# A sliding-window attention fused with a hard-swish MLP: a written TensorE order, one exp per block type, and a padded last tile

## The chip, the core and the metric

The kernel runs on one core of a Trainium2 chip. A core has TensorE (PE) for matrix products, VectorE (DVE), ScalarE (ACT) and GpSimd (POOL) for element-wise work, and SyncE (SP), which here only issues transfers between device memory and on-chip memory. Each engine works off its own queue in order. TensorE writes to psum, from which ACT and VectorE read. The metric is the device time of one execution in microseconds.

## The reference

Eight batches, eight heads, 576 positions, head size 64. Each position attends to itself and the 127 before it, with a bias that falls with the distance. The result, 4608 tokens of 512 values, goes through two matrix products with h * clip(h + 3, 0, 6) / 6 between them.

```python
scores = scale * np.matmul(q, k.transpose(0, 1, 3, 2))          # (8, 8, 576, 576)
mask = (rel >= 0) & (rel < window)                              # window = 128
scores = np.where(mask, scores + bias[None], -1000000000.0)
attn = np.exp(scores - np.max(scores, axis=-1, keepdims=True))
attn = attn / (np.sum(attn, axis=-1, keepdims=True) + 1e-09)
x = np.matmul(attn, v) ...                                      # (4608, 512)
h = x @ w_in                                                    # (4608, 2048)
g = h * np.clip(h + 3.0, 0.0, 6.0) / 6.0
return g @ w_out                                                # (4608, 512), float32
```

## The kernel before

The 576 positions are cut in tiles of 128; the fifth, last tile has 64 rows. With a window of 128, a tile of keys meets only its own tile of queries (the diagonal block) and the next one (the off-diagonal block). The unit of attention is a head pair: two heads fill the 128 partitions, 64 each. There are 32 pairs (8 batches of 4).

For a batch, SP loads q, k and v in 15 transfers (L80), POOL casts them to bf16 (L114 to L118). For a pair, TensorE transposes q and k (L127, 10 matmuls against an identity) and VectorE copies them out of psum (L130). Then two halves follow. In each TensorE makes scores (L142, L148: transposed, keys on partitions), diagonal and off-diagonal block of a key tile in one matmul of 256 columns; ACT takes the exp per block type (L159 to L169), two blocks of a type at once where it can, six passes to a head; POOL sets what lies outside the window to zero (L173 to L187); TensorE multiplies with v (L201 to L208), where v has a column of ones, so that column 64 is the sum; VectorE takes the reciprocal and multiplies (L213, L214). At last TensorE transposes the pair's result back (L223) and VectorE copies it into xT (L225), which holds all tokens with the model dimension on partitions.

The MLP (called MoE in the code) works on 9 groups of 512 tokens. An "up" (L235) is four matmuls of 512 columns, followed by a relu on ACT (L239) and a min-and-multiply on VectorE, which gives g (L240). A "down" (L251) is four matmuls of 512 columns from the group before, and every fourth down ends a tile of the output, which ACT or VectorE copies out of psum (L256, L258) and SP stores. There are 16 ups and 16 downs to a group; "unit" stands below for either.

The program writes attention of batch 0 first. Then it goes through the groups, and after each step's up and down it takes some pieces of the next batch's attention, by a generator that yields after each piece (L261 to L279). A scheduler then sets the order in each engine's queue and takes the liberty to move instructions past each other. In psum there are one score buffer (two banks), one av buffer, two transpose buffers, two up buffers (hps) and one down buffer (ops).

Of the kernel before, what the change touches and what calls it, by code (L numbers as in the profile page):

```python
# [18 lines left out]
def kernel(  # L19
# [18 lines left out]
    LAST = S - 4 * 128  # L38
    W = D + 1
# [18 lines left out]
    casts = ctx.enter_context(tc.tile_pool(name="casts", bufs=2))  # L58
    vpool = ctx.enter_context(tc.tile_pool(name="vpool", bufs=1))
    qkt = ctx.enter_context(tc.tile_pool(name="qkt", bufs=3))  # L60
    ppool = ctx.enter_context(tc.tile_pool(name="ppool", bufs=4))
    small = ctx.enter_context(tc.tile_pool(name="small", bufs=4))
    gpool = ctx.enter_context(tc.tile_pool(name="gpool", bufs=2))
    rpool = ctx.enter_context(tc.tile_pool(name="rpool", bufs=3))
    opool = ctx.enter_context(tc.tile_pool(name="opool", bufs=4))
# [5 lines left out]

    vbuf = [vpool.tile([128, NQ, H, W], BF16, name=f"vbuf{i}") for i in range(2)]

    def load(b):
        got = []
        for src, nm in ((q, "qf"), (k, "kf"), (v, "vf")):
            t = loads.tile([128, NQ, H, D], FP32, tag="ld", name=nm)
            for j in range(NQ):
                n = min(128, S - j * 128)
                nc.sync.dma_start(  # L80
                    out=t[:n, j, :, :],
                    in_=src[b, :, ds(j * 128, n), :].rearrange("h p d -> p h d"))
            got.append(t)
        return got

    first = load(0)
# [10 lines left out]
    for t in vbuf:  # L97
        nc.vector.memset(t[:, :, :, D:W], 1.0)

    for ks in range(n_ks):  # L100
        nc.gpsimd.dma_start(out=w_in_sb[:, ks, :], in_=moe_w_in[ts(ks, 128), :])
    for g in range(4):
        nc.gpsimd.dma_start(
            out=w_out_sb[:, ts(g, 4), :],
            in_=moe_w_out[ds(g * 512, 512), :].rearrange("(m p) d -> p m d", p=128))

    def attention(b):
        qf, kf, vf = first if b == 0 else load(b)
        qb = casts.tile([128, NQ, H * D], BF16, name="qb")
        kb = casts.tile([128, NQ, H * D], BF16, name="kb")  # L110
        vb = vbuf[b % 2]
        for src, dst in ((qf, qb), (kf, kb)):
            s = src.rearrange("p j h d -> p j (h d)")
            nc.gpsimd.tensor_copy(out=dst[:, 0:4, :], in_=s[:, 0:4, :])  # L114
            nc.gpsimd.tensor_copy(out=dst[:LAST, 4, :], in_=s[:LAST, 4, :])
        nc.gpsimd.tensor_copy(out=vb[:, 0:4, :, 0:D].rearrange("p j h d -> p (j h) d"),
                              in_=vf[:, 0:4, :, :].rearrange("p j h d -> p (j h) d"))
        nc.gpsimd.tensor_copy(out=vb[:LAST, 4, :, 0:D], in_=vf[:LAST, 4, :, :])  # L118
        yield

        for hp in range(NP):
            qkT = []
            for src, nm in ((qb, "qT"), (kb, "kT")):
                tp = ps_tp.tile([128, S], BF16, tag="tp", name="tp")
                for j in range(NQ):
                    n = min(128, S - j * 128)
                    nc.tensor.transpose(tp[:, ds(j * 128, n)], src[:n, j, ts(hp, 128)],  # L127
                                        ident[:n, :n])
                t = qkt.tile([128, S], BF16, tag=nm, name=nm)
                nc.vector.tensor_copy(out=t, in_=tp)  # L130
                qkT.append(t)
                yield
            qT, kT = qkT
            pt = []
            avs = small.tile([128, NQ, 2, D], BF16, tag="avs", name="avs")
            for st in range(2):
                sc = ps_sc.tile([128, 2, 512], FP32, tag="sc", name="sc")
# [123 lines left out]
    for _ in attention(0):  # L261
        pass
# [47 lines left out]
```

## Time and profile before

| | |
|---|---|
| median of 3 runs | 478.93 us (477.62 to 479.73) |
| the profiled execution | 478.99 us, span of its instructions 477.3 us |
| TensorE, matmuls | 403.3 us busy, 85% of the span, 2528 of them |
| VectorE, ACT, POOL | 41%, 46%, 32% |
| MoE up, MoE down | 576 matmuls of 512 columns each |

The span is the time from the first to the last instruction of the program. Matmuls are pipelined: one of 512 columns is shown with 0.38 us and the next starts 0.22 us later, so what a matmul costs is read from starts, not from durations.

### The profile page before, as it was taken

The page shows a single profiled execution, that of the slowest core. Times are in us where ns is not written, and L with a number is a line of the kernel's source. Part 1 is how long each engine was busy: PE and PEld are TensorE (multiplying, and loading weights), DVE is VectorE, ACT ScalarE, POOL GpSimd, SP SyncE. Part 2 cuts the span into 40 slices and gives each one's busy share as a digit, 9 for nine tenths or more (in the row PEclk, how much of TensorE's full clock was granted, in tenths as well). Part 3 has the DMA queues.
Part 4 walks back from the last instruction along what each step waited for, and adds up shares of the span by engine and source line. Part 5 has one row for each costly group of instructions (what it writes and reads, how often), then busy time and mean ns, then how long its engine had stood idle before and what let it go on. Part 6 is the DMA issues. An engine that isn't in the chain of part 4 may idle for free. (4 is left out here: it accounts for less than half of the span.)

```text
span 477.3 us, 6932 instructions
## 1 busy us (share of the span) xinstructions
PE 403.3 (85%) x2528; PEld 187.2 (39%) x2528; DVE 194.5 (41%) x470; ACT 219.9 (46%) x547; POOL 150.4 (32%) x255
## 2 busy tenths in 40 slices
PE   0003775998999999999999999999999999999976
PEld 0001432444344444444444444444444444444432
DVE  1000333554355545444544454454444544443420
ACT  1002335566565465546554655555545564444410
POOL 5025644454533622462245225522222222000000
PEclk9999999999799999999999999999999999999999
DMA  8999999500926877669409200000000000101111
GB/s 157 200 205 194 197 198 191 101 0 1 188 66 115 160 146 129 126 143 163 83 23 186 57 23 23 23 22 24 23 23 23 22 23 23 46 22 45 44 45 66
DMA packets 120419, 42.39 MB, mean 89 GB/s; under 512 B 113217, under 2 KB 115265, under 8 KB 120385
## 3 DMA queue, kind: packets, MB, share of 16 engines
q1 hardware_dynamic: 117696, 37.76, 40.8%
q0 software_dynamic: 2688, 4.19, 5.0%
q8 instruction: 19, 0.31, 0.3%
q14 instruction: 16, 0.12, 0.1%
HBM read 36.70 MB, written 9.44 MB: 97 GB/s over the span
## 5 line engine op out<-in xcount | busy, mean ns | idle before, releaser
L235 PE MATMUL hps<-xT,w_in_sb 128*128 128x512 bf16 x576 | 159.6, 388 | 3.3 <-DVE xT L225 2.1
L239 ACT ACTIVATE r<-hps,bias 128x512 f32<-128x512 f32 x144 | 98.2, 692 | 135.2 <-PE hps L235 135.0
L251 PE MATMUL ops<-w_out_sb,g 128*128 128x512 bf16 x576 | 155.0, 383 | 3.4 <-DVE osb L258 2.0
L240 DVE SCALAR_TENSOR_TENSOR g<-r,hps 128x512 bf16<-128x512 f32 x144 | 97.7, 683 | 114.1 <-ACT r L239 112.8
L173 POOL TENSOR_SCALAR_AFFINE_SELECT pp<-pp 128x512 bf16<-128x512 bf16 x64 | 40.6, 634 | 211.2 <-ACT pp L159 106.9
L159 ACT ACTIVATE pp<-sc,bias_d 128x256 bf16<-128x256 f32 x128 | 60.4, 472 | 99.2 <-PE sc L142 54.3
L251 PEld LDWEIGHTS <-g 128*128 128x128 bf16 x576 | 52.6, 98 | 62.3 <-issue 8.0
L235 PEld LDWEIGHTS <-w_in_sb 128*128 128x128 bf16 x576 | 51.3, 98 | 56.2 <-issue 8.3
L201 PE MATMUL av<-vbuf,pp 128*128 128x65 bf16 (+1 forms) x256 | 44.0, 208 | 5.3 <-DVE avs L214 2.9
L127 PE MATMUL tp<-ident,qb 128*128 128x128 bf16 (+1 forms) x160 | 21.9, 227 | 30.5 <-POOL qb L114 29.1
L205 PE MATMUL av<-vbuf,pp 128*128 128x65 bf16 x256 | 33.7, 203 | 14.2 <-POOL pp L173 11.6
L213 DVE RECIPROCAL rc<-av 128x4 f32<-128x4 f32 (+1 forms) x96 | 16.6, 172 | 69.0 <-PE av L208 49.5
L142 PE MATMUL sc<-qT,kT 64*128 64x256 bf16 (+1 forms) x256 | 35.0, 290 | 5.6 <-ACT pp L162 3.4
L214 DVE TENSOR_TENSOR avs<-av,rc 128x256 bf16<-128x256 f32 (+1 forms) x96 | 35.8, 372 | 1.4
L130 DVE COPY qT<-tp 128x576 bf16<-128x576 bf16 x32 | 14.5, 453 | 45.9 <-PE tp L127 45.8
L201 PEld LDWEIGHTS <-pp 128*128 128x128 bf16 (+1 forms) x256 | 23.3, 103 | 23.4 <-POOL pp L178 6.6
L205 PEld LDWEIGHTS <-pp 128*128 128x128 bf16 x256 | 19.8, 101 | 30.4 <-POOL pp L173 28.7
L162 ACT ACTIVATE pp<-sc,bias_o 128x256 bf16<-128x256 f32 x64 | 30.4, 476 | 0.0
L127 PEld LDWEIGHTS <-qb 128*128 128x128 bf16 (+1 forms) x160 | 12.8, 102 | 35.2 <-POOL qb L114 29.1
L223 PE MATMUL tp<-ident,avs 128*128 128x128 bf16 (+1 forms) x160 | 25.4, 226 | 0.0
L127 PE MATMUL tp<-ident,kb 128*128 128x128 bf16 (+1 forms) x160 | 19.2, 226 | 7.2 <-POOL kb L114 6.5
L142 PEld LDWEIGHTS <-kT 64*128 64x128 bf16 x256 | 10.6, 96 | 34.4 <-issue 19.6
(37 smaller groups left out, 294.7 us busy)
## 6 DMA issues: line engine op xcount, KB each, us to landing
out_dram<-osb SPq DMA_DIRECT2D x36, 256.0 KB, 2.0
qf<-in_q_dram SPq DMA_DIRECT2D x32, 256.0 KB, 5.3
kf<-in_k_dram SPq DMA_DIRECT2D x32, 256.0 KB, 5.1
vf<-in_v_dram SPq DMA_DIRECT2D x32, 256.0 KB, 5.0
w_in_sb<-in_moe_w_in_dram POOLq DMA_DIRECT2D x4, 512.0 KB, 10.6
w_out_sb<-in_moe_w_out_dram POOLq DMA_DIRECT2D x4, 512.0 KB, 20.6
qf<-in_q_dram SPq DMA_DIRECT2D x8, 128.0 KB, 5.0
kf<-in_k_dram SPq DMA_DIRECT2D x8, 128.0 KB, 5.4
```

Source lines behind the costliest of these rows:

```text
L127: nc.tensor.transpose(tp[:, ds(j * 128, n)], src[:n, j, ts(hp, 128)], ident[:n, :n])
L142: nc.tensor.matmul(sc[:, e, ds(j * 256, n)], lhsT=kT[e * D:(e + 1) * D, ts(kt, 128)], rhs=qT[e * D:(e + 1) * D, ds(kt * 128, n)], start=Tr ...
L159: nc.scalar.activation(out=pp[:, e, :, 0:128], in_=s4[:, :, 0:128], func=ACT.Exp, bias=bias_d[:, h:h + 1], scale=scale)
L162: nc.scalar.activation(out=pp[:, e, :, 128:256], in_=s4[:, :, 128:256], func=ACT.Exp, bias=bias_o[:, h:h + 1], scale=scale)
L173: nc.gpsimd.affine_select(out=dg, in_=dg, pattern=[[0, 4], [1, 128]], channel_multiplier=-1, base=0, compare_op=ALU.is_ge, fill=0.0)
L201: nc.tensor.matmul(av[:m, i, e, :], lhsT=src, rhs=vb[:, qt - 1, h, :], start=True, stop=False)
L205: nc.tensor.matmul(av[:m, i, e, :], lhsT=src, rhs=vb[:, qt, h, :], start=(qt == 0), stop=True)
L214: nc.vector.tensor_tensor(out=avs[:m, qts[lo]:qts[lo] + n, :, :], in0=av[:m, lo:lo + n, :, 0:D], in1=rc[:m, lo:lo + n, :, :].to_broadcast( ...
L235: nc.tensor.matmul(hps, lhsT=w_in_sb[:, ks, ts(ms, 128)], rhs=xT[:, ks, ts(nt, NT)], start=(ks == 0), stop=(ks == n_ks - 1))
L239: nc.scalar.activation(out=r6, in_=hps, func=ACT.Relu, bias=bias3[:, 0:1], scale=1.0 / 6.0)
L240: nc.vector.scalar_tensor_tensor(out=gts[nt][:, ms, :], in0=r6, scalar=1.0, in1=hps, op0=ALU.min, op1=ALU.mult)
L251: nc.tensor.matmul(ops[nt, sub], lhsT=gts[nt][:, ms, ts(sub, 128)], rhs=w_out_sb[:, ms, :], start=(ms == 0), stop=(ms == n_ms - 1))
```

## The change

On TensorE the order is now the program's own (`manual_schedule`); the other engines are scheduled as before. A loop over the 32 pairs and one more writes it: pieces of pair g (diagonal scores, off-diagonal scores), of pair g + 1 (transposes) and of pair g - 1 (values, transposing back), with eight units between them (`fill`). A unit is written only if its tokens' attention has been written before it; else `fill` returns with nothing. So no unit comes in the iterations 0 to 3, two ups at the end of 4, eight ups in 5, six in 6, none in 7, two units at the end of 8, and eight in each of the iterations 9 to 32. After the loop, 78 units are left.

Scores are made per block type: all four diagonal blocks of both heads (8 matmuls of 128 columns), later all off-diagonal ones with the last tile's own 64 columns (10 matmuls). So one exp of 512 columns serves a head's blocks of a type, and one of 64 columns the last tile. The last tile of q, k, v and of its probabilities is padded to 128 rows in buffers that are set up once, so that all transposes and value matmuls are 128 by 128. Values are taken for query tiles 0 to 2 and then 3 and 4. Batch 0 is loaded pair by pair (12 transfers each) and cast on VectorE; w_in is loaded by columns, in front of POOL's first selects, and w_out behind them. Pools of r6 and output buffers shrink to two.

In the rows of order below, a name on the left of `<-` is written. This is VectorE's queue before, at about the third batch: g is the product after an up, rc and avs belong to values, qT, kT and xT are copies out of the transpose buffers.

```order
L225 COPY xT<-tp 128x576
L240 SCALAR_TENSOR_TENSOR g<-r_2052,hps 128x512
L240 SCALAR_TENSOR_TENSOR g<-r_2077,hps 128x512
L213 RECIPROCAL rc<-av 128x4
L214 TENSOR_TENSOR avs<-av,rc 128x256
L258 COPY osb<-ops 128x512
L240 SCALAR_TENSOR_TENSOR g<-r_2116,hps 128x512
L213 RECIPROCAL rc<-av 128x4
L214 TENSOR_TENSOR avs<-av,rc 128x256
L213 RECIPROCAL rc<-av 64x2
L214 TENSOR_TENSOR avs<-av,rc 64x128
L130 COPY qT<-tp 128x576
```

And the same engine now, over one iteration in the same part of the program:

```order
L258 SCALAR_TENSOR_TENSOR g<-r_1997,hps 128x512
L258 SCALAR_TENSOR_TENSOR g<-r_2030,hps 128x512
L230 RECIPROCAL rc<-av 128x6
L231 TENSOR_TENSOR avs<-av,rc 128x384
L258 SCALAR_TENSOR_TENSOR g<-r_2057,hps 128x512
L230 RECIPROCAL rc<-av 128x4
L231 TENSOR_TENSOR avs<-av,rc 128x256
L158 COPY qT<-tp 128x640
L158 COPY kT<-tp 128x640
L258 SCALAR_TENSOR_TENSOR g<-r_2100,hps 128x512
L242 COPY xT<-tp 128x576
L258 SCALAR_TENSOR_TENSOR g<-r_2138,hps 128x512
```

A pair's values are now two pieces, of 384 and 256 elements, where they were three; one g stands ahead of each reciprocal. The next place is POOL's queue at the start, before:

```order
L101 DMA w_in_sb<-in_moe_w_in_dram 128x2048 x4
L103 DMA w_out_sb<-in_moe_w_out_dram 128x4x512 x4
L114 CAST qb<-qf 128x2048
L115 CAST qb<-qf 64x512
L114 CAST kb<-kf 128x2048
L115 CAST kb<-kf 64x512
L116 CAST vbuf_109<-vf 128x32x64
L118 CAST vbuf_109<-vf 64x8x64
L173 AFFINE_SELECT pp<-pp 128x4x128
```

And now:

```order
L119 DMA w_in_sb<-in_moe_w_in_dram 128x4x512 x4
L176 AFFINE_SELECT pd<-pd 128x512 x2
L204 AFFINE_SELECT po<-po 128x512
L125 DMA w_out_sb<-in_moe_w_out_dram 128x4x512
L204 AFFINE_SELECT po<-po 128x512
L207 AFFINE_SELECT p4buf_112<-p4buf_112 128x2x64
L125 DMA w_out_sb<-in_moe_w_out_dram 128x4x512
L176 AFFINE_SELECT pd<-pd 128x512 x2
L125 DMA w_out_sb<-in_moe_w_out_dram 128x4x512
L204 AFFINE_SELECT po<-po 128x512 x2
```

The casts of batch 0 have left POOL, and the four loads of w_out stand between the selects of the first two pairs.

```diff
+    def load_pair(got, b, hp):
+        for nm, src in srcs:
+            for h in (2 * hp, 2 * hp + 1):
+                nc.sync.dma_start(out=got[nm][:, 0:4, h, :],
+                                  in_=src[b, h, 0:512, :].rearrange("(t p) d -> p t d", p=128))
+                nc.sync.dma_start(out=got[nm][:LAST, 4, h, :], in_=src[b, h, 512:S, :])
...
+    for i in range(2):
+        nc.vector.memset(vbuf[i][:, :, :, D:W], 1.0)
+        nc.vector.memset(vbuf[i][64:128, 4, :, 0:D], 0.0)
+        nc.vector.memset(qbuf[i][64:128, 4, :], 0.0)
+        nc.vector.memset(kbuf[i][64:128, 4, :], 0.0)
+        nc.vector.memset(p4buf[i], 1.0)
...
+    def scores_diag(g):
...
+        for j in range(4):
+            for e in range(2):
+                r = slice(e * D, (e + 1) * D)
+                nc.tensor.matmul(sc[:, e, ts(j, 128)], lhsT=kT[r, ts(j, 128)],
+                                 rhs=qT[r, ts(j, 128)], start=True, stop=True)
+        pd = ppool.tile([128, 2, 4, 128], BF16, tag="pd", name="pd")
+        for e in range(2):
+            h = 2 * hp + e
+            nc.scalar.activation(out=pd[:, e, :, :].rearrange("p j c -> p (j c)"),
+                                 in_=sc[:, e, :], func=ACT.Exp,
+                                 bias=bias_d[:, h:h + 1], scale=scale)
...
+    def values(g, qts):
...
+        av = ps_av.tile([128, 3, 2, W], FP32, tag="av", name="av")
+        nq = len(qts)
+        for i, qt in enumerate(qts):
+            for e in range(2):
+                h = 2 * hp + e
+                if qt > 0:
+                    nc.tensor.matmul(av[:, i, e, :], lhsT=po[:, e, qt - 1, :],
+                                     rhs=vb[:, qt - 1, h, :], start=True, stop=False)
+                d = pd[:, e, qt, :] if qt < 4 else p4[:, e, :]
+                nc.tensor.matmul(av[:, i, e, :], lhsT=d, rhs=vb[:, qt, h, :],
+                                 start=(qt == 0), stop=True)
...
+    def fill(n):
+        for _ in range(n):
+            if at[0] == len(units):
+                return
+            nt, fn, step = units[at[0]]
+            if fn is moe_up and done[0] < NP * (min((nt * NT + NT - 1) // S, B - 1) + 1):
+                return
+            fn(nt if fn is moe_up else nt - 1, step)
+            at[0] += 1
...
+    with tc.manual_schedule(engines={mybir.EngineType.PE}):
+        prepare(0)
+        transposes(0)
+        for g in range(G + 1):
+            if g < G:
+                scores_diag(g)
+            if g + 1 < G:
+                prepare(g + 1)
+            fill(2)
+            if g > 0:
+                values(g - 1, (0, 1, 2))
+            fill(1)
+            if g > 0:
+                values(g - 1, (3, 4))
+            fill(1)
+            if g < G:
+                scores_off(g)
+            fill(1)
+            if g + 1 < G:
+                transposes(g + 1)
+            fill(1)
+            if g > 0:
+                back(g - 1)
+            fill(2)
+        fill(len(units))
```

`prepare(g)` casts pair g on VectorE in batch 0, casts a whole batch on POOL at the first pair of a later one, and writes the loads of the next batch at a batch's second pair.

## Rows read from the trace of the kernel before

**Rows 1.** The page: TensorE's busy share in 40 slices of 11.9 us, in tenths.
```profile
PE   0003775998999999999999999999999999999976
```
**Rows 2.** Timetable of POOL at the start: start us, duration us, instruction, idle before.
```profile
27.14 1.89 POOL L114 CAST qb<-qf 128x2048 bf16<-128x2048 f32 x1 [20.32 <-DMA qf<-in_q_dram]
30.48 0.61 POOL L115 CAST qb<-qf 64x512 bf16<-64x512 f32 x1 [1.45 <-DMA qf<-in_q_dram]
```
**Rows 3.** Timetable of SP's queue at the start: batch 0's q, batch 1's k.
```profile
0.81 15.76 SPq L80 DMA_DIRECT2D qf<-in_q_dram  x5
...
44.97 5.87 SPq L80 DMA_DIRECT2D kf<-in_k_dram  x5
```
**Rows 4.** Timetable of TensorE near the end of the second stage.
```profile
83.18 1.86 PE L235 MATMUL hps<-xT,w_in_sb 128*128 128x512 bf16 x4 [1.12 <-DVE g L240]
```
**Rows 5.** Busy time by stretch: length, PE, PEld, DVE, ACT, POOL; clock; DMA.
```profile
120.00:380.00 260.00, 251.00 (x1656) 116.97 (x1655) 125.88 (x303) 141.97 (x364) 93.41 (x161) 0.99 0.40 82
400.00:440.00 40.00, 40.00 (x186) 17.91 (x185) 17.60 (x29) 17.41 (x26) 0.00 (x0) 1.00 0.09 34
```
**Rows 6.** TensorE's groups from 120 to 380 us: count | busy us, mean ns.
```profile
L235 PE MATMUL hps<-xT,w_in_sb 128*128 128x512 bf16 x355 | 97.0, 383 | 0.0
L251 PE MATMUL ops<-w_out_sb,g 128*128 128x512 bf16 x344 | 96.2, 386 | 0.0
```
**Rows 7.** Timetable of TensorE in the steady stage.
```profile
204.09 0.39 PE L142 MATMUL sc<-qT,kT 64*128 64x256 bf16 x4
204.41 1.04 PE L235 MATMUL hps<-xT,w_in_sb 128*128 128x512 bf16 x4
...
210.04 0.20 PE L205 MATMUL av<-vbuf,pp 128*128 128x65 bf16 x1 [0.21 <-POOL pp L173]
210.08 0.20 PE L201 MATMUL av<-vbuf,pp 128*128 128x65 bf16 x1
...
211.25 0.22 PE L201 MATMUL av<-vbuf,pp 128*64 128x65 bf16 x1
211.40 0.21 PE L208 MATMUL av<-vbuf,p 64*64 64x65 bf16 x1
...
212.64 0.39 PE L127 MATMUL tp<-ident,qb 128*128 128x128 bf16 x4
212.86 0.28 PE L223 MATMUL tp<-ident,avs 128*128 128x128 bf16 x2
```
**Rows 8.** Timetable of ACT in the steady stage: an exp, a relu.
```profile
205.67 0.48 ACT L162 ACTIVATE pp<-sc,bias_o 128x256 bf16<-128x256 f32 x1
206.02 0.70 ACT L239 ACTIVATE r<-hps,bias 128x512 f32<-128x512 f32 x1
```
**Rows 9.** Timetable of VectorE in the steady stage: g, then a pair's last values.
```profile
210.48 0.69 DVE L240 SCALAR_TENSOR_TENSOR g<-r,hps 128x512 bf16<-128x512 f32 x1 [0.28 <-ACT r L239]
211.65 0.18 DVE L213 RECIPROCAL rc<-av 128x4 f32<-128x4 f32 x1 [0.49 <-PE av L208]
211.87 0.42 DVE L214 TENSOR_TENSOR avs<-av,rc 128x256 bf16<-128x256 f32 x1
```
**Rows 10.** The page: weight loads of the scores; loads of k.
```profile
L142 PEld LDWEIGHTS <-kT 64*128 64x128 bf16 x256 | 10.6, 96 | 34.4 <-issue 19.6 <-DVE kT L130 5.5 <-DVE xT L225 2.5
...
kf<-in_k_dram SPq DMA_DIRECT2D x32, 256.0 KB, 5.1
```
**Rows 11.** Stretch with TensorE alone: length, PE; clock; DMA.
```profile
122.00:124.00 2.00, 2.00 (x9) 0.50 1.28 257
```
**Rows 12.** The chain that ended last, its end: start us, us, what.
```profile
454.64 0.02 issue
...
456.72 3.63 PE ops L251 x16
...
461.01 3.63 PE ops L251 x16
...
473.34 0.69 DVE osb L258
```

More of the change, by code (lines that the diff above doesn't have):

```diff
@@ L38 @@
     LAST = S - 4 * 128
+    SP = NQ * 128
     W = D + 1
@@ L80, in load @@
                 nc.sync.dma_start(
-                    out=t[:n, j, :, :],
+                    out=got[nm][:n, j, :, :],
                     in_=src[b, :, ds(j * 128, n), :].rearrange("h p d -> p h d"))
-            got.append(t)
-        return got
-    first = load(0)
+    got0 = new_loads()
+    for hp in range(NP):
+        load_pair(got0, 0, hp)
     make_identity(nc, ident)
@@ L228, with transposes @@
-    gts = {}
+                              in_=got["vf"][:, 0:4, :, :].rearrange("p j h d -> p (j h) d"))
+        nc.gpsimd.tensor_copy(out=vb[:LAST, 4, :, 0:D], in_=got["vf"][:LAST, 4, :, :])
+    st = {}
+    def transposes(g):
+        b, hp = divmod(g, NP)
+        for src, nm in ((qbuf[b % 2], "qT"), (kbuf[b % 2], "kT")):
+            tp = ps_tp.tile([128, SP], BF16, tag="tp", name="tp")
+            for j in range(NQ):
+                nc.tensor.transpose(tp[:, ts(j, 128)], src[:, j, ts(hp, 128)], ident)
+            t = qkt.tile([128, SP], BF16, tag=nm, name=nm)
+            nc.vector.tensor_copy(out=t, in_=tp)
+            st[g, nm] = t
@@ new lines, in values @@
+    def values(g, qts):
+        b, hp = divmod(g, NP)
+        vb = vbuf[b % 2]
+        pd, po, p4 = st[g, "pd"], st[g, "po"], p4buf[g % 2]
+        av = ps_av.tile([128, 3, 2, W], FP32, tag="av", name="av")
+        nq = len(qts)
+        for i, qt in enumerate(qts):
+            for e in range(2):
+                h = 2 * hp + e
+                if qt > 0:
[4 more added lines that the diff above has]
+                                 start=(qt == 0), stop=True)
+        if qts[0] == 0:
+            st[g, "avs"] = small.tile([128, NQ, 2, D], BF16, tag="avs", name="avs")
+        rc = small.tile([128, 3, 2, 1], FP32, tag="rc", name="rc")
+        nc.vector.reciprocal(rc[:, 0:nq, :, :], av[:, 0:nq, :, D:W])
+        nc.vector.tensor_tensor(
+            out=st[g, "avs"][:, qts[0]:qts[0] + nq, :, :], in0=av[:, 0:nq, :, 0:D],
+            in1=rc[:, 0:nq, :, :].to_broadcast([128, nq, 2, D]), op=ALU.mult)
@@ L230, in moe_up, with back @@
+    def back(g):
+        b, hp = divmod(g, NP)
+        avs = st[g, "avs"]
+        tp = ps_tp.tile([128, SP], BF16, tag="tp", name="tp")
+        for j in range(NQ):
+            nc.tensor.transpose(tp[:, ts(j, 128)],
+                                avs[:, j, :, :].rearrange("p e d -> p (e d)"), ident)
+        nc.vector.tensor_copy(out=xT[:, hp, ds(b * S, S)], in_=tp[:, 0:S])
+        done[0] = g + 1
+    done = [0]
+    gts, ops = {}, {}
     def moe_up(nt, ms):
@@ L241, in moe_up @@
                                        op0=ALU.min, op1=ALU.mult)
-    ops = {}
     def moe_down(nt, step):
```

236 lines of the change are left out of this document (89 added, 147 removed).

## The prediction, made before the changed kernel was run

> **What bounds the kernel now.** I read the 40 slices first, then the timetables of the start, the groups by stage, and one steady stretch matmul by matmul. The slices show three stages [rows 1]: TensorE does nothing for some 29 us, works at 30 to 80% until about 85 us, and is at 90% or more to the end. In the first stage it waits for data: POOL's first cast waits 20.32 us for the DMA of q [rows 2], and SP needs 15.76 us to issue five loads beside the weight loads where 5.87 do later [rows 3]. In the second, head pairs run one after the other, and TensorE's clock is low: four 512-column matmuls last 1.86 us [rows 4], where four of the steady stage last 1.04 [rows 7].
>
> In the third stage TensorE is busy, but not full. A pure MoE stretch has 186 matmuls in 40.00 us [rows 5], 0.86 us per unit of four. From 120 to 380 us there are 1656 matmuls [rows 5], of which 355 + 344 = 699 are MoE [rows 6]. These are 175 units, 151 us; the other 109 us go to 957 attention matmuls. A head pair has 43 (15 transposes, 10 scores, 18 values), so 22.3 pairs at 4.9 us each. The timetable shows why [rows 7]: full value matmuls start 0.04 us apart and four full transposes take 0.22, but a value matmul of the 64-row last tile holds TensorE for 0.15; four score matmuls of 256 columns hold it for 0.32; and at 210.04 it has stood empty for POOL's select. The other engines are at 55% or less there [rows 5]. So the bound is TensorE's own order.
>
> **The change, part by part.** All durations are from the profiled execution (478.99 us, span 477.3), which lies on the median of 478.93.
>
> *TensorE's work for a pair.* 15 full transposes at 0.055 us are 0.8; 18 full value matmuls at 0.04 are 0.7 [rows 7]. Scores come in groups of 8 and 10, and two heads run side by side in 64 rows each. Two such steps of 256 columns hold 0.32 us; 512 columns of MoE alone are 0.215, so 0.1 is the change of shape on the way out, and I take as much on the way in. A step of 128 columns is then 0.055, rounded to 0.06; 7 of these, 2 short ones of 0.04 and two groups' changes of 0.2 give 0.9. The pair needs 2.4 us. Bounds for a score step are 0.04 (the pace of value matmuls) and 0.15 (that of the partial tile): 2.3 to 3.2 us. I take the row that it is nearest to, the 256-column step.
>
> Beside that row stands a rule. The Trainium skill (TensorE: Matmul & The Clock Gate, "Part 3: Packing small matmuls — row/col tiling", "The mechanism") says that a weight load overlaps running matmuls only when its row group differs. Every score step reloads both row groups; by this rule twice as many steps would bring their weight loads into the open, some 28 us over the run by the trace's length of a load.
>
> *Waits that the written order leaves.* One iteration holds eight units, 6.9 us, and one pair: diagonal scores, up, down, values 0 to 2, up, values 3 and 4, down, off-diagonal scores, up, transposes, down, back, up, down. Values 3 and 4 write the single av buffer, which VectorE must have read. After the diagonal scores ACT does two exps, then the first up's relu. An exp of 256 columns holds ACT for 0.35 us and lasts 0.48, a 512-wide pass lasts 0.70 [rows 8], so I estimate 0.57 for 512. The relu ends 2.3 us after the diagonal scores began, and VectorE's g (0.69 [rows 9]) ends at 3.0; in VectorE's queue g stands ahead of the reciprocal. The values are done at 2.6. Reciprocal and product take 0.22 + 0.42 us at 256 elements [rows 9], some 0.8 at 384, so av is free at 3.85, where values 3 and 4 are due at 3.3: 0.55 us of wait. The first down after a finished output tile waits some 0.2 us on average for the copy out of the one buffer, the first up of a batch about half a microsecond for xT. That is 0.9 per pair singly; as a wait gives time to the next, I take 0.8. The ends: nothing (VectorE free in time), and 2.5, which is what the pair holds now beyond its 2.4.
> What hides the rest: exps and selects have six units and the pieces between, some 6.4 us, before their values are asked for. POOL's casts (1.89 and 0.61 [rows 2]) can stand in between; with two of them the cover is gone.
> An iteration is 6.9 + 2.4 + 0.8 = 10.1 us, against 6.9 + 4.9 = 11.8 now.
>
> *The start.* The first pair is loaded by itself and cast on VectorE, and w_out is issued behind POOL's first selects, so TensorE starts well before 29 us. But in its order the transposes of batch 1 stand ahead of the last values of batch 0, and the first unit behind these. So k of batch 1 decides. The bytes ahead of it (q, k and v of batch 0, the weights, q of batch 1) are those of now; SP has issued it by 50.84 us [rows 3], and a load lands 5.1 after its issue [rows 10]: 55. With 48 transfers for batch 0 in place of 15 I allow 50 to 60. Then POOL casts (1.89 + 0.61), and transposes, diagonal scores, values 0 to 4, off-diagonal scores, transposes and back follow at the low clock, 7.5 us with their copies: the first unit starts at 65. Sixteen ups follow with two pairs: 13.8 us of matmuls, 4.8 for the pairs, 1.5 for the low clock, and six because an up's psum buffer (two) is held through relu (0.70) and g (0.69), so that ups alone come 1.28 us apart: 91. The next two pairs have no units, since the next up needs all of batch 1, and take their chain of exp, select, values and copy, 9 us for both; then two units: 102. The clock may fall there: it is granted at 0.50, 1.2 of 2.4 GHz, from 122 to 124 us now [rows 11]. I add 3 us for half the pace.
>
> *The end.* Ups and downs alternate strictly; the down behind a finished tile waits some 0.3 us for the copy at ten places: 3 us. The last 16 downs keep their waits, 456.72 - 454.64 = 2.1 us before them and 4.29 - 3.63 = 0.7 three times between [rows 12]: 4.1. From the last matmul at 473.34 to the span's end are 4.0, to the run's end 1.7 more.
>
> *Off the path.* Wider exps (ACT is at 55%), memsets (in the DMA wait), longer copies of the padded tile (VectorE is at 48% [rows 5]). If this cover goes, the wait above grows by what they add, under 0.2 us per pair.
>
> *Sum.* 102 + 3 + 24 iterations x 10.1 (242) - 2 for what the last two leave out + 78 units left x 0.86 (67) + 3 + 4.1 + 5.7 = 425. I take 421: the clock's 3 us are not certain, nor are all the singly added waits. Start 92 and wait 0.3 give about 400; start 107 and wait 1.4, 444.
>
> **Rivals.**
> 1. The waits hide. TensorE is then bound by its own 9.3 to 9.4 us per iteration: 24 x 0.75 less, 403. For it: VectorE is half idle. Against: one av buffer, and g ahead of the reciprocal.
> 2. The written order cannot step round a late producer, as a scheduler's can. With selects behind POOL's casts the values wait, and an iteration is 11.2 to 12: 447 to 466. For it: the cover that two casts use up. Against: the order puts casts one to three pairs ahead, and POOL's queue is a third busy [rows 5].
> 3. Weight loads in the open. Each of the 9 score steps pays one load, 96 ns by the mean [rows 10]: 0.86 x 32 = 28 us, 449. Against: at 204.09 two steps take little over the time of their columns, loads included, so these were hidden. The rule named above makes this rival; the trace so far speaks against it.
> 4. Slower. At each of the seven batch changes TensorE stands until the next batch is cast: three casts of 1.89 + 0.61 on POOL are 7.5 us, and the copies and scores behind them 1 more: 60 us in all, 481. It decides from 8.3 us per change. For it: POOL's queue stops at a cast whose load is late, and the transposes stand fast in TensorE's order. Against: a batch's loads are issued in 18 us (three times 5.87) of an iteration's four times 10.
>
> **How the numbers follow.** Forecast 0.58, rival 1 0.15, rival 2 0.18, rival 3 0.06, rival 4 0.03. The forecast's own range is 408 to 436; with most of rival 1 and half of 2 and 3 it is 400 to 446. Within 0.5% (2.4 us, about what a measurement can tell from no change) is 0.01; slower is rival 4, 0.03; faster 0.96.
>
> **What would show it.** Value matmuls 0.04 us apart to the last tile, score steps of 0.06, iterations of 10 us with one wait of half a microsecond before values 3 and 4 that VectorE's avs ends; the first MoE matmul at 60 to 70 us, behind the cast of batch 1's k; a stretch of some 9 us without MoE before 100. I am wrong on the start if the first MoE matmul comes before 55 or after 75, on the waits if TensorE stands before values 0 to 2 (POOL) or before ups, and on the work if score steps take over 0.1 us.

## The result, and the profile after

The median of four runs is 419.54 us (419.14 to 421.72), beside 478.27 us (477.28 to 479.73) for the kernel before: a ratio of 0.878, with a 95% interval of 0.874 to 0.882. The prediction was 421. The profiled execution took 419.74 us, its span 417.7.

The page of the kernel after, TensorE's 40 slices (10.4 us each) and busy time, which answers to [rows 1]:

```profile
PE   0141618878999899989998999899899999999985
...
PE 338.9 (81%) x2739; PEld 175.2 (42%) x2784; DVE 201.5 (48%) x438; ACT 198.5 (48%) x355; POOL 145.1 (35%) x217
```

TensorE starts earlier, stands at 10 to 60% until about 60 us, and behind that it is still the busiest engine but less full than it was: an 8 comes back every four slices or so.

TensorE's timetable of the kernel after at the start (start us, duration us, instruction, idle before):

```profile
8.95 0.72 PE L156 MATMUL tp<-ident,qbuf 128*128 128x128 bf16 x5 [8.95 <-DVE qbuf L132]
...
62.30 0.84 PE L156 MATMUL tp<-ident,kbuf 128*128 128x128 bf16 x5 [4.07 <-POOL kbuf L142]
...
69.19 2.60 PE L253 MATMUL hps<-xT,w_in_sb 128*128 128x512 bf16 x7 [0.22 <-issue]
...
91.90 0.40 PE L168 MATMUL sc<-qT,kT 64*128 64x128 bf16 x8
```

The first transposes come at 9 us instead of some 29, but the first unit only at 69.19: the transposes of batch 1's k at 62.30 stand ahead of it in the written order. At 91.90 begins the first of the two iterations without units.

POOL and SP of the kernel after at the start, which answer to [rows 2, 3]; first POOL, then SP:

```profile
60.35 1.89 POOL L142 CAST kbuf<-kf 128x2048 bf16<-128x2048 f32 x1 [2.46 <-DMA kf<-in_k_dram]
```

```profile
51.58 5.83 SPq L93 DMA_DIRECT2D kf<-in_k_dram  x5
```

The five loads of batch 1's k are issued 6.6 us later than before (51.58 against 44.97), and the cast waits for them.

One iteration of the steady stage, TensorE after, which answers to [rows 7]:

```profile
202.83 0.40 PE L168 MATMUL sc<-qT,kT 64*128 64x128 bf16 x8
203.16 1.04 PE L253 MATMUL hps<-xT,w_in_sb 128*128 128x512 bf16 x4
...
204.90 0.23 PE L225 MATMUL av<-vbuf,pd 128*128 128x65 bf16 x2
...
205.20 1.03 PE L253 MATMUL hps<-xT,w_in_sb 128*128 128x512 bf16 x4
206.59 0.20 PE L222 MATMUL av<-vbuf,po 128*128 128x65 bf16 x1 [0.36 <-DVE avs L231]
...
206.84 1.02 PE L267 MATMUL ops<-w_out_sb,g 128*128 128x512 bf16 x4
207.79 0.37 PE L189 MATMUL sc<-qT,kT 64*128 64x128 bf16 x8
208.00 0.19 PE L193 MATMUL sc<-qT,kT 64*128 64x64 bf16 x2
...
209.00 0.44 PE L156 MATMUL tp<-ident,qbuf 128*128 128x128 bf16 x5
209.28 0.44 PE L156 MATMUL tp<-ident,kbuf 128*128 128x128 bf16 x5
...
212.53 0.40 PE L168 MATMUL sc<-qT,kT 64*128 64x128 bf16 x8
```

This iteration lasts 212.53 - 202.83 = 9.70 us. Ten values go in 0.30 us (204.90 to 205.20), the eight with the last tile in 0.25; five transposes in 0.28; four score steps in 0.21. The one hole is at 206.59. The record shows 0.36 of idle, since it counts from a matmul's modelled end; by starts, four matmuls of 512 columns from 205.20 would be through at 206.07 (0.216 each), so 0.52 is lost.

VectorE at that place, which answers to [rows 9] and says why:

```profile
205.14 0.69 DVE L258 SCALAR_TENSOR_TENSOR g<-r,hps 128x512 bf16<-128x512 f32 x1 [1.96 <-ACT r L257]
...
205.97 0.56 DVE L231 TENSOR_TENSOR avs<-av,rc 128x384 bf16<-128x384 f32 x1
```

The first values were made by 205.4; the reciprocal stood behind g, which ended at 205.83, and avs frees the av buffer at 206.53. ACT's queue, which answers to [rows 8], had two exps, 1.26 us together, ahead of the relu that g waits for:

```profile
203.27 1.26 ACT L173 ACTIVATE pd<-sc,bias_d 128x512 bf16<-128x512 f32 x2 [0.81 <-PE sc L168]
```

What TensorE waited for from 110 to 320 us (instruction, line, releaser: us in total, times, longest):

```profile
PE av L222 <- DVE avs L231: 7.6, 21, 0.4
PE hps L253 <- DVE xT L242: 4.7, 5, 0.9
```

Two waits, both foreseen, make nearly all of it: av in every iteration, xT at every batch change. None is POOL's. A third that the prediction had, for the copy of a finished output tile, is not among them. By stretch, which answers to [rows 5, 11] (length; busy time of PE, of PEld, which are TensorE's weight loads, of DVE, ACT, POOL; clock; DMA):

```profile
93.00:98.00 5.00, 3.56 (x47) 2.75 (x48) 3.22 (x8) 2.76 (x7) 4.91 (x7) 0.69 1.10 210
...
120.00:280.00 160.00, 148.05 (x1307) 76.38 (x1329) 87.93 (x186) 92.31 (x169) 72.25 (x105) 1.00 0.53 109
```

The clock fell in the iterations without units: 0.69 is a mean over the two levels, 2.4 and 1.2 GHz, while TensorE was busy for 3.56 of 5 us. In the steady stage TensorE stands for 160 - 148.05 = 11.95 us.

The end of the chain, which answers to [rows 12]:

```profile
395.14 0.02 issue
...
397.22 3.63 PE ops L267 x16
...
413.89 0.69 DVE osb L274
```

It is as before: 2.08 us between 395.14 and 397.22, then four tiles, and 3.8 us from 413.89 to the end of the span.

### The profile page after: what moved, and what is told of

Read it like the earlier page. It is cut to its first block, busy times and chain, and to the rows that moved or that the text cites. A ratio compares the mean times of both kernels' runs of the same rounds, so it can differ in the third digit from the quotient of the medians.

```text
span 417.7 us, 7115 instructions
## 1 busy us (share of the span) xinstructions
PE 338.9 (81%) x2739; PEld 175.2 (42%) x2784; DVE 201.5 (48%) x438; ACT 198.5 (48%) x355; POOL 145.1 (35%) x217
## 4 chain that ended last, share of the span: by engine, by line
PE 46%; DVE 15%; ACT 14%; issue 11%; DMA 8%; SPq 4%; POOL 1%; DVEq 0%; POOLq 0%; ACTq 0%
PE ops L267 22%; PE hps L253 13%; ACT r L257 8%; DMA vf<-in_v_dram 6%; DVE g L258 5%; DVE avs L231 4%; DVE osb L274 3%; ACT pd L173 3%; PE tp L156 2%; PE sc L168 2%; PE av L222 2%; PE sc L189 2%; ACT p4buf L202 2%; SPq L87 2%; DMA kf<-in_k_dram 2%
## 5 line engine op out<-in xcount | busy, mean ns | idle before, releaser
L176 POOL TENSOR_SCALAR_AFFINE_SELECT pd<-pd 128x512 bf16<-128x512 bf16 x64 | 39.8, 644 | 96.9 <-ACT pd L173 96.9
L204 POOL TENSOR_SCALAR_AFFINE_SELECT po<-po 128x512 bf16<-128x512 bf16 x64 | 40.4, 634 | 79.0 <-ACT po L199 75.7
L199 ACT ACTIVATE po<-sc,bias_o 128x512 bf16<-128x512 f32 x64 | 44.0, 687 | 39.3 <-PE sc L193 39.3
L173 ACT ACTIVATE pd<-sc,bias_d 128x512 bf16<-128x512 f32 x64 | 40.5, 683 | 43.1 <-PE sc L168 43.1
L222 PE MATMUL av<-vbuf,po 128*128 128x65 bf16 x256 | 26.1, 201 | 15.4 <-DVE avs L231 15.3
L231 DVE TENSOR_TENSOR avs<-av,rc 128x384 bf16<-128x384 f32 x64 | 31.4, 491 | 2.0
L222 PEld LDWEIGHTS <-po 128*128 128x128 bf16 x256 | 18.9, 102 | 29.3 <-DVE avs L231 29.0
L225 PE MATMUL av<-vbuf,pd 128*128 128x65 bf16 x256 | 25.0, 201 | 0.0
L225 PEld LDWEIGHTS <-pd 128*128 128x128 bf16 x256 | 20.0, 101 | 7.2 <-issue 0.8
L202 ACT ACTIVATE p4buf<-sc,bias_d 128x64 bf16<-128x64 f32 x64 | 20.2, 315 | 0.0
## 6 DMA issues: line engine op xcount, KB each, us to landing
w_in_sb<-in_moe_w_in_dram POOLq DMA_DIRECT2D x4, 512.0 KB, 10.4
w_out_sb<-in_moe_w_out_dram POOLq DMA_DIRECT2D x4, 512.0 KB, 10.1
```

The costliest lines, as they stand in the source:

```text
L173: nc.scalar.activation(out=pd[:, e, :, :].rearrange("p j c -> p (j c)"), in_=sc[:, e, :], func=ACT.Exp, bias=bias_d[:, h:h + 1], scale=scale)
L176: nc.gpsimd.affine_select(out=pd[:, e, :, :], in_=pd[:, e, :, :], pattern=[[0, 4], [1, 128]], channel_multiplier=-1, base=0, compare_op=AL ...
L199: nc.scalar.activation(out=po[:, e, :, :].rearrange("p j c -> p (j c)"), in_=sc[:, e, :], func=ACT.Exp, bias=bias_o[:, h:h + 1], scale=scale)
L204: nc.gpsimd.affine_select(out=po[:, e, :, :], in_=po[:, e, :, :], pattern=[[0, 4], [-1, 128]], channel_multiplier=1, base=-1, compare_op=A ...
L222: nc.tensor.matmul(av[:, i, e, :], lhsT=po[:, e, qt - 1, :], rhs=vb[:, qt - 1, h, :], start=True, stop=False)
L225: nc.tensor.matmul(av[:, i, e, :], lhsT=d, rhs=vb[:, qt, h, :], start=(qt == 0), stop=True)
```

## The experiments

Every time is a median of four runs, the ratio is to the kernel before, measured beside it, with its 95% interval. After itself is 419.5 and 0.878.

| run | us (range) | ratio |
|---|---|---|
| e1_sched | 395.16 (393.94 to 396.92) | 0.827 (0.824 to 0.830) |
| e2_nopad | 447.74 (446.16 to 448.62) | 0.936 (0.933 to 0.940) |
| e4_two | 407.63 (406.69 to 409.96) | 0.854 (0.850 to 0.858) |
| e5_wout | 415.35 (413.67 to 416.17) | 0.869 (0.864 to 0.873) |
| e6_xt | 424.37 (423.92 to 424.62) | 0.888 (0.884 to 0.892) |
| e7_oldstart | 414.82 (413.98 to 418.62) | 0.869 (0.865 to 0.874) |
| e9_sched_nopad | 427.17 (425.93 to 428.17) | 0.894 (0.889 to 0.898) |
| e10_sched_old | 395.70 (395.58 to 396.18) | 0.828 (0.824 to 0.832) |
| e11_halves | 397.89 (396.66 to 398.56) | 0.833 (0.829 to 0.836) |
| e12_unpiped | 425.14 (424.53 to 426.69) | 0.891 (0.887 to 0.894) |
| e13_written | 402.81 (401.84 to 403.80) | 0.844 (0.840 to 0.847) |
| e14_sched_wout | 396.04 (395.80 to 397.07) | 0.830 (0.827 to 0.833) |

### What the written order is worth: e1_sched

The same program, with TensorE's queue left to the scheduler like the others:

```diff
-    with tc.manual_schedule(engines={mybir.EngineType.PE}):
+    if True:
```

> The changed kernel with TensorE's written order taken away: the scheduler orders TensorE again, all else stays (pair-wise loads, padded tile, 512-wide exps). Theory (the gain is in two parts, less TensorE work per pair through the padded tile and grouped scores, and fewer waits and shape changes through the written order): a pair holds TensorE for 2.4 us plus some 1.3 of waits and broken groups, 425 to 440 us. Rival A (the written order makes all of the gain): 455 us or more. Rival B (the order makes none of it, the work per pair all): 413 to 422 us.

It is 24 us faster than the kernel after, and below every expectation: the written order by itself costs time. TensorE's busy time in e1_sched:

```profile
PE 339.4 (87%) x2735; PEld 175.0 (45%) x2784; DVE 200.7 (51%) x438; ACT 198.0 (50%) x355; POOL 144.4 (37%) x217
```

The work is the same, 339.4 us beside 338.9; what is gone are the holes. TensorE in e1_sched at the place where the kernel after waits for av:

```profile
207.89 1.03 PE L253 MATMUL hps<-xT,w_in_sb 128*128 128x512 bf16 x4
208.75 0.59 PE L267 MATMUL ops<-w_out_sb,g 128*128 128x512 bf16 x2
209.27 0.20 PE L222 MATMUL av<-vbuf,po 128*128 128x65 bf16 x1
```

From the end of one group of values to the next are 1.38 us, as in the kernel after (205.20 to 206.59, 1.39). But there it is an up and a hole, here an up and half a down. And its stretches:

```profile
90.00:100.00 10.00, 9.74 (x106) 5.54 (x107) 6.97 (x17) 7.62 (x16) 9.60 (x14) 1.00 0.99 178
...
120.00:280.00 160.00, 158.22 (x1388) 81.28 (x1413) 93.33 (x196) 97.07 (x178) 74.90 (x109) 1.00 0.57 111
```

It stands for 1.78 us in these 160, against 11.95: 0.64 us for every 10, and with some 213 us of such iterations in the kernel after (110 to 323) that is 13.5 us. The rest comes from the start, by the MoE matmuls up to 110 us, first of the kernel after, then of e1_sched:

```profile
L253 PE MATMUL hps<-xT,w_in_sb 128*128 128x512 bf16 x75 | 20.5, 393 | 2.3 <-DVE g L258 1.7 <-issue 0.4
L267 PE MATMUL ops<-w_out_sb,g 128*128 128x512 bf16 x13 | 3.5, 379 | 0.0
```

```profile
L253 PE MATMUL hps<-xT,w_in_sb 128*128 128x512 bf16 x92 | 25.5, 386 | 2.1 <-DVE g L258 1.1 <-DVE xT L242 0.3 <-issue 0.2
L267 PE MATMUL ops<-w_out_sb,g 128*128 128x512 bf16 x29 | 8.2, 379 | 0.1
```

These are 88 against 121, 22 units against 30: 8.25 x 0.86 = 7 us, and some of the pairs' work is ahead too. From 90 to 100 us, where the kernel after has no unit to run and a lower clock, e1_sched is at 9.74 of 10 and 1.00: it went on with batch 1's pairs between the ups (297 matmuls from 62 to 92 us, where the kernel after has 228), and so is not left without units.

### Which places of the order cost: e4_two, e6_xt

e4_two puts a second unit between the two groups of values, taken from ahead of the first group:

```diff
                 prepare(g + 1)
-            fill(2)
+            fill(1)
             if g > 0:
                 values(g - 1, (0, 1, 2))
-            fill(1)
+            fill(2)
```

> One unit is moved from ahead of values 0 to 2 to behind them, so two units stand between the two value groups that share the av buffer. Theory (0.52 us of wait in each iteration for VectorE's read of av, because g stands ahead of the reciprocal and one unit covers only 0.86): the wait goes, 27 x 0.5 = 13 us less, 405 to 409 us. Rival (the wait moves to another place, such as values 0 to 2 for POOL's selects, asked for 0.86 us earlier): 417 to 420 us.

12 us faster, as the theory had it. The wait for av is gone from the steady stage, and the one for xT stays; TensorE's waits from 110 to 320 us:

```profile
PE hps L253 <- DVE xT L242: 3.6, 5, 0.7
```

e6_xt writes the transposing back directly behind the transposes, so that xT is ready earlier at a batch change:

```diff
                 transposes(g + 1)
-            fill(1)
             if g > 0:
                 back(g - 1)
+            fill(1 if g > 8 else 0)
             fill(2)
```

> The changed kernel with the transposing back written one unit earlier, so that at a batch change a down stands between it and the up that reads xT. Theory (0.9 us of wait for VectorE's copy of xT at each of the six batch changes): 4 to 5 us less, 414 to 416 us. Rival (the wait is only moved, since another piece then waits for VectorE): 418 to 421 us.

It is 5 us slower, where the theory had a gain and the rival no change. The wait for xT did go, but 15 transposes in a row need three transpose buffers where there are two, and the third waits for VectorE's copy of qT in every iteration, while the wait for av stays. TensorE's new wait, from 110 to 320 us:

```profile
PE tp L240 <- DVE qT L158: 6.1, 20, 0.3
```

By starts the new wait costs 0.47 us in every pair (five transposes from 211.47 would be through at 211.75, and the next start at 212.22); what was won is 0.9 per batch, 0.22 per pair. The difference, 0.25 x 24 iterations = 6 us, is near the 4.8 that were measured. The unit between transposes and back had covered that buffer.

### What the start is worth: e5_wout, e7_oldstart

e5_wout holds w_out's loads until batch 1's k is cast, by a tiny copy that they have to follow:

```diff
         for g in range(4):
+            nc.gpsimd.tensor_copy(out=w_out_sb[0:64, 4 * g, 0:1], in_=kbuf[1][0:64, 4, 0:1])
             nc.gpsimd.dma_start(
...
-            if hp == 3:
-                load_weights_out()
         elif hp == 0:
             cast_all(got[b], b)
+            if b == 1:
+                load_weights_out()
```

> The changed kernel with the four loads of w_out held back behind POOL's cast of batch 1's k (a one-column copy from that tile into w_out makes them wait). Theory (k of batch 1 decides the start, and the weights' bytes stand ahead of it): k lands some 10 us sooner, the first unit comes at 58 to 61 us, total 408 to 413 us. Rival (the time is lost again to v of batch 1 and the loads of batch 2, which come behind w_out instead): 416 to 421 us.

The cast of k and the first unit of e5_wout, POOL and then TensorE:

```profile
52.67 1.89 POOL L143 CAST kbuf<-kf 128x2048 bf16<-128x2048 f32 x1 [3.57 <-DMA kf<-in_k_dram]
```

```profile
61.43 1.68 PE L254 MATMUL hps<-xT,w_in_sb 128*128 128x512 bf16 x7
```

Both 7.7 us earlier than after (60.35 and 69.19): w_out's loads did delay k. But the run gains only 4 us, between the two expectations. The rest is lost before the steady stage, whose first iteration begins at 99.4, 3.8 us earlier than after (103.2). The rival's reason holds for this part: batch 2's loads now come beside and behind w_out's (SP is held for 15.71 us by those of q, 6.75 after). POOL's cast of batch 2's q in e5_wout, then one of TensorE's waits from 61 to 100 us (total, times, longest):

```profile
76.12 1.89 POOL L143 CAST qbuf<-qf 128x2048 bf16<-128x2048 f32 x1 [10.43 <-DMA qf<-in_q_dram]
```

```profile
PE av L223 <- POOL po L205: 2.6, 4, 1.3
```

POOL stands at this cast for 10.43 us, with selects behind it in its queue, and the values wait for selects at four places (78.65, 79.24, 91.48, 92.07), 2.6 us in all. The kernel after has no such wait there. From 92 to 100 us the granted clock is 0.57 besides; how the 3.8 us divide between the two was not tried.

e7_oldstart takes back the whole start: batch 0 in 15 transfers cast on POOL, w_in by rows, both weights at once.

```diff
-    for hp in range(NP):
-        load_pair(got0, 0, hp)
+    load_all(got0, 0)
...
-                out=w_in_sb[:, :, ts(g, 512)],
-                in_=moe_w_in[:, ts(g, 512)].rearrange("(k p) f -> p k f", p=128))
+                out=w_in_sb[:, g, :], in_=moe_w_in[ts(g, 128), :])
...
-            cast_pair(got[0], 0, hp, nc.vector)
-            if hp == 1:
+            if hp == 0:
                 load_weights_in()
-            if hp == 3:
                 load_weights_out()
+                cast_all(got[0], 0)
```

> The changed kernel with the start of before: batch 0 in 15 whole transfers, both weights issued at once by rows, casts of batch 0 on POOL. Theory (the first unit waits for k of batch 1, and the bytes ahead of it are the same either way): TensorE starts near 38 us in place of 9, yet the total stays within 4 us, 416 to 424 us. Rival (the early start is worth what it shows): 20 us or more slower, 435 to 450 us.

4.7 us faster than the kernel after, on the theory's side and beyond it. TensorE's first work and first unit in e7_oldstart:

```profile
31.41 0.84 PE L154 MATMUL tp<-ident,qbuf 128*128 128x128 bf16 x5 [31.41 <-POOL qbuf L140]
...
66.10 1.74 PE L251 MATMUL hps<-xT,w_in_sb 128*128 128x512 bf16 x7
```

TensorE begins 22 us later than after (8.95), and its first unit comes 3 us sooner. The transfers of the first 60 us say why it can: busy share of the 16 DMA engines in 40 slices of 1.5 us, and what they moved, in the kernel after, then in e7_oldstart:

```profile
DMA  0489999999999565699899999997526569999999
...
DMA packets 28447, 10.19 MB, mean 170 GB/s; under 512 B 24349, under 2 KB 28445, under 8 KB 28445
```

```profile
DMA  0699999999999999999999999999999999995899
...
DMA packets 31946, 11.59 MB, mean 193 GB/s; under 512 B 29384, under 2 KB 31432, under 8 KB 31944
```

The kernel after leaves the DMA engines half idle twice, where no weights are loading and SP alone has to keep them busy; SP in the kernel after in the second of these gaps:

```profile
44.67 0.59 SPq L85 DMA_DIRECT2D vf<-in_v_dram  x1
45.30 0.51 SPq L87 DMA_DIRECT2D vf<-in_v_dram  x1
```

A head's two transfers, 128 and 16 KB, hold SP from 44.67 to 45.81, and the next starts at 45.86: 144 KB in 1.19 us are 124 GB/s, where the queues move some 200. So loading pair by pair gets the first pair sooner and all that follows later: 1.4 MB less by 60 us are 7 us at that pace. In the kernel after, batch 1's k is the load that decides. In e7_oldstart SP issues it from 44.11, 7.5 us sooner, and its cast waits for no DMA:

```profile
57.13 1.90 POOL L140 CAST kbuf<-kf 128x2048 bf16<-128x2048 f32 x1
```

This cast stands behind selects of batch 0, and from 37.53 to the first unit TensorE goes through pairs without a wait for batch 1's loads or casts. So there it is the late beginning that sets the first unit, which gains 3 us, not 7. (e7_oldstart changes w_in's rows and the time of w_out's loads as well; how the 7 us divide between these was not tried.)

### What the rest of the change is worth: e2_nopad, e9_sched_nopad, e11_halves, e12_unpiped

e2_nopad takes the last tile back to 64 rows in transposes, scores, exps, selects and values, which gives POOL a select and VectorE a reciprocal and a product more per pair:

```diff
-                nc.tensor.transpose(tp[:, ts(j, 128)], src[:, j, ts(hp, 128)], ident)
+                n = min(128, S - j * 128)
+                nc.tensor.transpose(tp[:, ds(j * 128, n)], src[:n, j, ts(hp, 128)], ident[:n, :n])
...
-                    nc.tensor.matmul(av[:, i, e, :], lhsT=po[:, e, qt - 1, :],
+                    nc.tensor.matmul(av[:m, i, e, :], lhsT=po[:, e, qt - 1, 0:m],
```

> The changed kernel with the last tile back at 64 rows in the transposes, the scores' last block, the values, the reciprocal and the product; order, exps and loads stay. Theory (partial tiles hold TensorE: 4 value matmuls at 0.146 in place of 0.031 us, 3 transposes at 0.17 more each, 1.0 us per pair, in the open in the 24 iterations): 443 us, at least 436. Rival A (the written order's waits take it up): under 428 us. Rival B (the gain was all in the padding): 470 us or more.

28 us slower, as expected. TensorE in e2_nopad, the last tile's values and the transposes of q and k:

```profile
200.84 0.22 PE L227 MATMUL av<-vbuf,po 128*64 128x65 bf16 x1
...
201.42 1.04 PE L274 MATMUL ops<-w_out_sb,g 128*128 128x512 bf16 x4
...
203.71 0.52 PE L157 MATMUL tp<-ident,qbuf 128*128 128x128 bf16 x5
204.16 0.53 PE L157 MATMUL tp<-ident,kbuf 128*128 128x128 bf16 x5
```

The four values of the last tile hold 0.58 us (200.84 to 201.42), where full ones take 0.12, and five transposes 0.45 instead of 0.28. Per pair that is 0.46 + 3 x 0.17 = 0.97 us, 31 over 32 pairs. The wait for av is as it was (6.9 us in 19 places from 110 to 320 us), so VectorE's two passes more are not what costs. The padded tile computes twice the rows and is faster.

e9_sched_nopad is the same under the scheduler (e2_nopad's edit with e1_sched's):

```diff
-    with tc.manual_schedule(engines={mybir.EngineType.PE}):
+    if True:
...
-                    nc.tensor.matmul(av[:, i, e, :], lhsT=po[:, e, qt - 1, :],
+                    nc.tensor.matmul(av[:m, i, e, :], lhsT=po[:, e, qt - 1, 0:m],
```

> The scheduler's order (as in the run without the written one) with the last tile back at 64 rows. Theory (the padding saves TensorE time whoever sets the order): 26 to 30 us above the scheduler's 395, 421 to 426 us. Rival (the scheduler puts partial tiles where TensorE would wait anyway): 395 to 408 us.

427.2 - 395.2 = 32 us for the padding, some more than expected, and 447.7 - 427.2 = 20.5 for the written order in a kernel without it: neither effect rests on the other.

e11_halves gives scores, exps and selects back their two halves (a diagonal and an off-diagonal block in one matmul, exps of 256 columns), under the scheduler:

```diff
-            nc.scalar.activation(out=pd[:, e, :, :].rearrange("p j c -> p (j c)"),
-                                 in_=sc[:, e, :], func=ACT.Exp,
-                                 bias=bias_d[:, h:h + 1], scale=scale)
+            nc.scalar.activation(out=pd[:, e, ts(x, 2), :], in_=s4[:, :, 0:128], func=ACT.Exp,
+                                 bias=bias_d[:, h:h + 1], scale=scale)
+            nc.scalar.activation(out=po[:, e, ts(x, 2), :], in_=s4[:, :, 128:256], func=ACT.Exp,
+                                 bias=bias_o[:, h:h + 1], scale=scale)
...
-    with tc.manual_schedule(engines={mybir.EngineType.PE}):
+    if True:
```

> The scheduler's order, with scores, exps and selects by halves as before (10 score matmuls of up to 256 columns, 8 exps of 256 and 2 of 64 per pair; 8 selects of 256 and one of 128); pad, start and the program's pipelining stay. Theory (one exp per block type is off the path, since ACT holds 0.6 us more per pair at half load): 393 to 400 us. Rival (grouping the scores and exps is what moved the pair from 4 to 2.4 us): 415 us or more.

The scores and exps per block type are worth at most a few us, as the theory had it: 2.7 by the medians, with ratios whose intervals overlap (0.829 to 0.836 and 0.824 to 0.830). ACT was not the bound.

e12_unpiped keeps the pieces, but the program writes those of one pair one behind the other, with units between; casts and loads move back with them:

```diff
+        for g in range(G):
+            prepare(g)
+            transposes(g)
             fill(1)
+            scores_diag(g)
             fill(1)
+            scores_off(g)
+            fill(2)
+            values(g, (0, 1, 2))
             fill(1)
+            values(g, (3, 4))
             fill(1)
+            back(g)
             fill(2)
```

> The scheduler's order, with a pair's pieces written one behind the other (transposes, diagonal, off-diagonal, values, back, with units between) in place of pieces of three pairs in turn; work, pad and start stay. Theory (the remaining 50 us of the gain under the scheduler, beyond the padding's 32, come from units standing between dependent pieces of a pair, and the program's order is what the scheduler goes by): 410 to 440 us. Rival (the scheduler finds the overlap by itself): 393 to 400 us.

30 us slower. A scheduler that may move instructions does not make up for a program that asks for a pair's values just behind its scores; TensorE's longest wait in e12_unpiped, 110 to 320 us, and a stretch of it:

```profile
PE av L225 <- POOL pd L176: 5.5, 22, 0.7
```

```profile
120.00:280.00 160.00, 149.58 (x1301) 73.54 (x1299) 87.36 (x186) 90.75 (x167) 74.74 (x106) 1.00 0.55 109
```

This wait is a sixth of the loss. In all TensorE stands for 10.42 us of these 160, against 1.78 in e1_sched, and the run is behind before that: by 110 us its record has 532 matmuls, e1_sched's 670. How the rest of the 30 divides was not followed. The expectation, 410 to 440, was too wide to be missed.

### Putting the better parts together: e10_sched_old, e13_written, e14_sched_wout

e10_sched_old is e1_sched with e7_oldstart's start, e13_written is the written order with e4_two's and e5_wout's edits, e14_sched_wout is e1_sched with w_out held back and w_in by rows:

```diff
 e10_sched_old
-    for hp in range(NP):
-        load_pair(got0, 0, hp)
+    load_all(got0, 0)
...
-    with tc.manual_schedule(engines={mybir.EngineType.PE}):
+    if True:
```

> The scheduler's order with the start of before (batch 0 in whole transfers, weights at once by rows, casts on POOL). Theory (the early start gives nothing, and rows of 8 KB for w_in let batch 1's k land sooner, as with the written order, where the old start was 4.7 us faster): 388 to 394 us. Rival (the scheduler can use the early pairs, having no batch 1 transposes in its way): 398 us or more.

```diff
 e13_written
+            nc.gpsimd.tensor_copy(out=w_out_sb[0:64, 4 * g, 0:1], in_=kbuf[1][0:64, 4, 0:1])
...
-            fill(2)
+            fill(1)
             if g > 0:
                 values(g - 1, (0, 1, 2))
-            fill(1)
+            fill(2)
```

> The written order with two edits that were each faster: two units between the value groups, and w_out behind batch 1's k. Theory (both savings are at separate places and add): 419.5 - 12 - 4, 402 to 405 us, still above the scheduler's 395, since units may not come in iterations 0 to 3 and 7 and xT's wait stays. Rival (they share a slack): 407 us or more.

```diff
 e14_sched_wout
+            nc.gpsimd.tensor_copy(out=w_out_sb[0:64, 4 * g, 0:1], in_=kbuf[1][0:64, 4, 0:1])
...
-    with tc.manual_schedule(engines={mybir.EngineType.PE}):
+    if True:
```

> The scheduler's order, w_out behind batch 1's k, and w_in by rows of 8 KB. Theory (the start still waits for batch 1's k, and the scheduler can use units earlier): 388 to 392 us. Rival (the loads of batch 2, which come later by as much, take it back): 394 to 397 us.

e10_sched_old and e14_sched_wout measure the same as e1_sched (395.7 and 396.0 beside 395.2), the first between its two expectations and the second as its rival had it: with a scheduler the start of the change is worth nothing, and neither is the earlier k. e13_written is the sum of its two parts, as expected, and 17 us faster than the kernel after, but a written order with both mended is still 7.6 us behind the scheduler's. e1_sched, which beats the kernel before by 17%, is the best version found, and differs from the change in one line.

**The account.** From 478.3 to e1_sched's 395.2 are 83 us. Taken away singly under the scheduler, the padding is worth 32, the pipelined writing 30, scores and exps per type at most 3, the start nothing: 65. Some 18 us are not accounted for by single edits. Effects that need each other, the grouping of the values (0 to 2, then 3 and 4) and the pattern of units are candidates; none was tried alone. From 395.2 the written order goes back to 419.5: 24 us, 13.5 in the steady stage and some 10 at the start.

## Why the prediction was right, step by step

- **The pair's work, 2.4 us.** Right: values at 0.03 us to the last tile (forecast 0.04), five transposes 0.28 (0.055 each, as forecast), a score step 0.05 (0.06), 0.09 for the change of shape ahead of the scores (206.84 + 4 x 0.216 = 207.70, and they start at 207.79) and 0.12 behind them (203.16 - 202.83 less four steps). Rival 3, weight loads in the open, is out: four steps with eight loads of 94 ns took 0.21 us. The rule that made it stands in the Trainium skill (TensorE: Matmul & The Clock Gate, Part 3, "The mechanism"): a weight load overlaps running matmuls only when its row group differs. This trace does not agree with that: the values' loads take all 128 rows and 98 ns each, and ten values with their loads went in 0.30 us.
- **Waits, 0.8 per iteration.** Right in the sum and in its main part: 0.52 for av (forecast 0.55, ended by avs with g ahead of the reciprocal, as written). The two small terms were mis-sized, one each way: 0.9 for xT at a batch change (forecast about half a microsecond), and none for the copy of a finished output tile (forecast 0.2 in each iteration). The prediction also named a stand before ups as a sign of being wrong; it came, at the batch changes, where the forecast itself had it. The 22 iterations from 103.2 to 322.7 took 9.98 us each, against 10.1. Rival 4, 8.3 us at a batch change, is out with the 0.9.
- **The start.** The cause was right, batch 1's k. Its term was mis-sized: k landed at 60.3, as the cast at 60.35 that waits for it shows, just past the upper bound of 60, not at 55. The step argued that the bytes ahead of k are those of now, and so took SP's issue time from [rows 3]; the bytes are the same, but the DMA engines were not kept full (10.19 MB by 60 us, 11.59 in e7_oldstart with 15 large transfers). So the first unit came at 69.19, not 65. The 16 ups then took 22.7 us, not 26, and the next iteration began at 91.90, forecast 91. One miss hid the other.
- **The stretch without units.** They are missing from 91.90 on, and the steady iterations begin at 103.2, forecast 102 and 3 for the clock; it fell to 0.69 there.
- **The end.** 2.08 us, four tiles with 0.7 between, 3.8: as forecast. The 3 us for copies at ten places were too much: the record has three such places between 340 and 395 us (354.18, 368.53, 382.88), of 0.37 us each.
- **What it had wrong.** Rival 2, a written order that cannot step round a late producer, was priced as a wait for POOL's selects, at 447 to 466 us, and set against the forecast. In the kernel after the values never waited for the selects (in e5_wout they did, for 2.6 us). But the mechanism was in the forecast itself, at another place and size: the 0.8 per iteration that the forecast called the price of one av buffer and the late xT are waits that a scheduler steps round with the same buffers (e1_sched: 1.78 us in 160), and the stretch without units is one that it fills. The step that failed is "the bound is TensorE's own order", read as if the new order could only mend it. The time came out since the new order's waits had been counted one by one; that the change would be better by 24 us without its title's first half was not in the text. Rival 1's 403, in which the waits hide, is near what e13_written measured, but partly by chance: covering the av wait alone gave 407.6 (e4_two), and the rest came with e5_wout's edit.

## What to carry to other kernels

A written order on the bound engine is to be weighed part by part: writing the program pipelined, making tiles of one shape and fixing the queue are three edits, and here the first two gained 30 and 32 us under a scheduler while the third lost 24. Where a queue is fixed by hand, count for each single buffer the time from its last write to its release against the work that stands between, and give it that much work: one more unit between the two values was worth 12 us. An engine that begins 20 us sooner gains nothing where it then stands for the next batch's data.

## What the runs showed of the hardware that was not expected

- Value matmuls of 64 rows or 64 columns start 0.145 us apart on average, full ones of the same 65 columns 0.03 (e2_nopad and after). The trace of before had the first figure; that it holds for a whole tile's transposes too, 0.45 for five with one short where 0.28 is the full price, had been left out.
- A transfer of 16 KB holds SP's queue for 0.51 us, one of 128 KB for 0.59, where no weights load. At this pace the two, in turn, feed 124 GB/s into engines that move 200.
- An idle time in the record is short of the loss, since the end of a matmul is modelled: 0.36 shown at 206.59, 0.52 by starts.
